# Block operands summed by an accumulating DMA from GpSimd instead of by VectorE, in a three-stage kernel on one Trainium2 core

## The chip, the core and the metric

The kernel runs on one core of a Trainium2 chip. The metric is device time in microseconds of one execution. Three runs of the kernel before gave 957.30, 958.35 and 959.70 us, a median of 958.35. One more execution was recorded by the profiler: it took 953.06 us, of which its trace spans 951.3.

## The reference

The program computes three stages in a row: linear attention with random features, a dense mixture of four experts (all tokens go through all experts, weighted by a probability), and a small second mixture with soft slots.

```python
# attention: q, k, v are (4, 8, 576, 64)
h = x @ omega.T - sum(x * x) / 2;  phi = exp(h - max(h)) / sqrt(128)
kv = phi(k).T @ v;  num = phi(q) @ kv;  den = phi(q) @ sum(phi(k))
x = num / (den + 1e-6)                   # then 2304 tokens x 512

# first mixture: w1 (4, 512, 1024), w2 (4, 1024, 512)
p = domain_probs / (domain_probs.sum(-1) + 1e-9)
for e in range(4):
    out += p[:, e:e+1] * (maximum(x @ w1[e], 0) @ w2[e])

# second mixture: 8 experts of 4 slots each
d = softmax over tokens of (out @ phi);  slots = d.T @ out
slot_out = maximum(slots @ w1[e], 0) @ w2[e] for each expert's slots
result = softmax over slots of (out @ phi) @ slot_out
```

All inputs and the output are float32.

## The kernel before

The middle stage takes most of the time: on TensorE it runs from about 152 us to about 890. It works in the type float32r. Each operand is kept as a high part and a low part (the rest that the high part leaves), and a product of two operands is three matmuls: high by high, high by low, low by high.

The work of this stage is cut into units. A unit is one of 8 weight groups (4 experts, 2 halves of the hidden layer each) with one of three blocks of 768 tokens: 24 units, numbered `u`, of weight group `G = u // 3` and block `b = u % 3`. From unit 3 on, the first layer and everywhere the second layer are done by a scheme with 7 products instead of 8 (the names I1, I2, I6, I5, I7, I3, I4 are the products in their order). Each product is 12 matmuls of 128 x 128 by 128 x 384. In units 0, 1 and 2 the first layer is done plainly, with 8 products (`plain1`), because the 7-product scheme needs four combined operands of each token block that are not there yet.

These combined operands are prepared beside the plain units, from the four sub-blocks of each token block, named `KH[0]` to `KH[3]`. For each block there are three sorts of step:

- W (`whole`): the high and low parts of a sub-block are added, to give it as one float32 array, `blocks[b, kh]` of 128 x 768. Four per block.
- T (`block_sum`): four differences of sub-blocks, in place, on VectorE. T 0 needs KH[0] and KH[2].
- S (`block_split`): the result is split again into a high part (cast on ScalarE) and a low part (a subtraction on VectorE), and both go to DRAM (`xt`) two ticks later, by two DMAs that ScalarE issues. Four per block.

The order is written out by hand. TensorE alternates a first-layer product of unit `u` (`plain1` or `product1`) with a second-layer product of unit `u - 1` (`product2`), and after each of them the table in `prep_steps` is asked for steps. Its key is `(u, n)`: even `n` is behind the matmuls of first-layer product `n / 2` of unit `u`, odd `n` behind second-layer product `(n - 1) / 2` of unit `u - 1`. A step that the table puts there is queued at that point on its engine. All engines take their instructions in order, so a step that waits holds up all that is queued behind it on that engine.

On VectorE the steps stand between the evacuations: ReLU with the token's weight (`scaled`, L595), the combinations of the hidden layer (L665, L734), its low parts (`split_low`, L659), and the sums of second-layer products (`evacuate2`, L806). ScalarE casts the high parts (L655) and copies some second-layer products out of PSUM (L808). GpSimd combines the weights (`weight_sum`, L419) and forms their low parts behind ScalarE's casts (`weight_split`, L437 and L438). SP issues the loads: operands `x` (L462) go three ahead through a ring of three buffers, so that a load waits until the operand three places earlier has been read by all its readers.

In the kernel before, W has two forms. For block 0, `fetch` loads the high and the low parts with eight DMAs from SP, near the end of attention, and VectorE adds them (L501). For blocks 1 and 2, VectorE adds the two halves of the operand that the ring holds for the plain products (L498), so those additions are readers of the ring's buffers too.

Of the kernel before, what the change touches and what calls it, by code (L numbers as in the profile page):

```python
# [9 lines left out]
F32 = mybir.dt.float32  # L10
F32R = mybir.dt.float32r
AF = mybir.ActivationFunctionType
ALU = mybir.AluOpType
# [4 lines left out]
B, H, S, D = 4, 8, 576, 64  # L18
# [22 lines left out]
def f32(ap):  # L41
    return ap.bitcast(F32)
# [3 lines left out]
def body(ctx: ExitStack, tc: tile.TileContext, ql, kl, vl, om, dp, wl, phi, w2l, out):  # L46
    nc = tc.nc
# [20 lines left out]
    def bank(tag, name):  # L68
        g = groups[tag]
        turns[tag] = turns.get(tag, -1) + 1  # L70
        n = g[turns[tag] % len(g)]
        return banks[n].tile([P, 512], F32, name=name, tag=f"k{n}", bufs=1)
# [29 lines left out]
    xd = [[dram.tile([P, 2, 2, NP, 2 * P], F32R, name=f"xd{b}_{h}") for h in range(2)] for b in range(XB)]  # L102
# [214 lines left out]
    def step(i):  # L317
        if i + 4 < n_seq:
            load(i + 4)
        to_dram()  # L320
        kind = seq[i][0] if i < n_seq else ""
        if begun(i, "q") and begun(i - 1, "q"):
            kind = "qq"
        for n in orders[kind].split():
            if n == "W":
                if early:
                    early.pop(0)()
                continue
            f, lag, kinds, *rest = work[n]
            if n == "P1" and i in (1, 2):  # L330
                keep_warm(10 if i == 1 else 7, "d")
            if begun(i - lag, *kinds) and not (n == "S" and i == 0):
                f(i - lag, *rest)
            if n == "M0" and i == 0:
                squares(0)
        if i == 0:
            split(2)
            split(3)
# [33 lines left out]
    I1, I2, I6, I5, I7, I3, I4 = range(7)  # L372
    w1s, w2s, hs, xs_, stage, lo_t, acc1, acc2, blocks, x2 = {}, {}, {}, {}, {}, {}, {}, {}, {}, []
# [14 lines left out]
    spare = [w1e.tile([P, 4, 2 * TH], F32, name="whole0", tag="w1x")]  # L388

    def raw_load(which, G):  # L390
        c = slice(0, DM) if which == "w1" else slice(DM, 2 * DM)
        r = stg.tile([P, 2, 2, 2, HD], F32, name=f"raw{which}", tag="raw")
        nc.sync.dma_start(
            out=r.rearrange("p j a h d -> p (j a) (h d)"),
            in_=wl[G * GJ:(G + 1) * GJ, :, c].rearrange("j p c -> p j c"),
        )
        stage[which, G] = r, stg.tile([P, 4, 2, HD], F32, name=f"T{which}", tag="T")
# [25 lines left out]
    def plain_terms():  # L423
        r, _ = stage["w1", 0]
        stage["w1", 0] = {i: r[:, :, k, m, :] for i, (k, m) in PLAIN.items()}
# [19 lines left out]
    def htile(i, lo, dt=F32R):  # L445
        n = HT[i] + ("l" if lo else "h")
        return hp.tile([P, 2 * TH], dt, name=n, tag=n)

    def three(t):
        return t.rearrange("p (a c) -> p a c", a=NP)  # L450
# [17 lines left out]
            load_operand(*ring[n])  # L468

    KH = ((0, 0), (1, 0), (0, 1), (1, 1))  # L470
    lows = {}

    def fetch():
        for n, (kh, i) in enumerate(zip(KH, (I5, I6, I3, I4))):
            k, half = kh
            blocks[0, kh] = spare[0][:, n]
            lows[kh] = htile(i, 1, F32)
            src = xd[0][half][:, k]
            nc.sync.dma_start(out=three(blocks[0, kh]), in_=f32(src[:, 0]))
            nc.sync.dma_start(out=three(lows[kh]), in_=f32(src[:, 1]))  # L480

    def place(b, kh):
        k, half = kh
        if b == 1:
            if kh == (0, 0):
                stage["xr"] = x2p.tile([P, 4, 2 * TH], F32, name="xr", tag="x2_2")
            blocks[b, kh] = stage["xr"][:, 2 * half + k]
        else:
            if k == 0:
                stage["xr", half] = prep.tile([P, 4, 512], F32, name="xr", tag=f"pre{half}")  # L490
            blocks[b, kh] = stage["xr", half].rearrange("p a c -> p (a c)")[:, k * 2 * TH:(k + 1) * 2 * TH]

    def whole(b, kh):
        if b:
            place(b, kh)
            hi, lo = xs_[b, kh]
            out = three(blocks[b, kh])
            nc.vector.tensor_tensor(out=out, in0=f32(hi), in1=f32(lo), op=ALU.add)  # L498
        else:
            a = blocks[b, kh]  # L500
            nc.vector.tensor_tensor(out=a, in0=a, in1=lows[kh], op=ALU.add)  # L501

    def block_sum(b, n):
        b11, b21, b12, b22 = (blocks[b, kh] for kh in KH)
# [30 lines left out]
        after(2, ("xt", b, i), keep)  # L535

    def prep_steps():
        W, T, S = whole, block_sum, block_split
        return {
            (0, 6): [(W, 0, KH[0])],  # L540
            (0, 8): [(W, 0, KH[1])],
            (0, 10): [(W, 0, KH[2]), (W, 0, KH[3])],
            (0, 12): [(T, 0, 0), (T, 0, 1)],
            (0, 14): [(T, 0, 2), (T, 0, 3)],
            (1, 4): [(W, 1, KH[0])],
            (1, 5): [(S, 0, I6)],
            (1, 6): [(W, 1, KH[1])],
            (1, 7): [(W, 1, KH[2])],
            (1, 8): [(W, 1, KH[3])],
            (1, 9): [(S, 0, I5)],  # L550
            (1, 10): [(T, 1, 0)],
            (1, 11): [(S, 0, I7), (T, 1, 1)],
            (1, 12): [(S, 0, I4)],
            (1, 13): [(T, 1, 2)],
            (2, 4): [(W, 2, KH[0])],
            (2, 6): [(W, 2, KH[1])],
            (2, 7): [(T, 1, 3)],
            (2, 8): [(W, 2, KH[2])],
            (2, 9): [(S, 1, I5)],
            (2, 10): [(S, 1, I4)],  # L560
            (2, 11): [(W, 2, KH[3])],
            (2, 12): [(S, 1, I7)],
            (2, 13): [(S, 1, I6)],
            (3, 5): [(T, 2, 0)],
            (3, 6): [(T, 2, 1)],
            (3, 7): [(T, 2, 2)],
            (3, 8): [(T, 2, 3)],
            (3, 13): [(S, 2, I6)],
            (4, 6): [(S, 2, I5)],
            (4, 7): [(S, 2, I7)],  # L570
            (4, 12): [(S, 2, I4)],
        }

    steps = prep_steps()

    def prep_one(u, n):
# [5 lines left out]
    def load_share(u):  # L582
        G, b = units[u]
        t = prb[u] = (
            prep.tile([P, 2, TH], F32, name="prb", tag=f"prb{u % 2}") if u else
            htile(I4, 0, F32).rearrange("p (a t) -> p a t", a=2)
        )
        nc.sync.dma_start(
            out=t.rearrange("p a (n t) -> p (a n) t", n=NP),
            in_=prd[TB * b:TB * b + TB, GROUPS[G][0], :].partition_broadcast(P),  # L590
        )
# [261 lines left out]
    for i in range(n_seq + 5):  # L853
        step(i)
        if i == 2:
            nc.sync.dma_start(out=phis, in_=phi.rearrange("(k p) s -> p k s", p=P))
            nc.vector.tensor_reduce(out=psum, in_=pr, axis=AX.X, op=ALU.add)
            nc.vector.tensor_scalar_add(psum, psum, 1e-9)
            nc.vector.reciprocal(out=psum, in_=psum)
            nc.vector.tensor_tensor(out=pr, in0=pr, in1=psum.to_broadcast([P, NT, E]), op=ALU.mult)  # L860
        if i == 3:
            tp = bank("d", "prt")
            nc.tensor.transpose(tp[0:NT * E, 0:P], pr.rearrange("p t e -> p (t e)"), ident)
            prs = pa.tile([P, P], F32, name="prs", tag="prs", bufs=1)
            nc.scalar.copy(out=prs[0:NT * E], in_=tp[0:NT * E, 0:P])
            nc.sync.dma_start(out=prd.rearrange("t e p -> (t e) p"), in_=prs[0:NT * E])
        if i == 14:
            load_share(0)
        if i == 19:
            raw_load("w1", 0)  # L870
            plain_terms()
        if 20 <= i < 20 + GJ:
            weight_split("w1", 0, (I1, I2, I6, I4)[i - 20])
        if i == 24:
            raw_load("w2", 0)
        if i == last_key + 2:
            groups.update({"b": [3, 4, 5], "c": [6]})
        if i == n_seq - 4:
            for n in range(3):
                load_operand(*ring[n])  # L880
        if i == n_seq - 2:
            fetch()
        if i == n_seq - 1:
            pa1.release()
            w2p = pool("w2p")
            lt = pool("lt")
            for n in range(4):
                weight_sum("w2", 0, n)
            groups.update({"b": [3, 4], "d": [5], "c": [6]})
            psH.release()  # L890
            pp["1"] = pool("ps1", space=PSUM, side="right")
        if n_seq <= i:
            for o in range(2 * (i - n_seq), min(7, 2 * (i - n_seq + 1))):
                weight_split("w2", 0, o)
# [189 lines left out]
    n = NB - 1  # L1084
# [243 lines left out]
```

## Time and profile before

| what | us |
|---|---|
| median of three runs | 958.35 (957.30 to 959.70) |
| profiled execution, whole | 953.06 |
| its span in the trace | 951.3 |
| TensorE busy | 932.7 (98%) |
| VectorE busy | 752.3 (79%) |
| ScalarE busy | 428.5 (45%) |
| GpSimd busy | 353.7 (37%) |
| chain that ended last | TensorE 86%, VectorE 6%, DMA 3%, ScalarE 2% |

An engine's busy time is the sum of its instructions, with overlaps counted once. TensorE is busy nearly all the time, so the end is set by its work and by the places where it stands still. Those places are found in the timeline of TensorE, where a bracket behind a row gives the idle time before it and the instruction that ended it. The granted TensorE clock is 1.00 of full speed in every stretch from 140 to 850 us, so it plays no part in units 0 to 5.

### The profile page before, as it was taken

The numbers are of one execution on the slowest core, as the hardware profiler recorded it, in microseconds if no ns is written. First come the engines' busy times: TensorE is split into PE (matmuls) and PEld (weight loads), VectorE is DVE, ScalarE is ACT, GpSimd is POOL, SyncE is SP. The second block draws the span as 40 slices with busy tenths as digits, with TensorE's granted clock in tenths as the row PEclk, the third lists the DMA queues.
The fourth block names the chain that finished last, engine by engine and source line by source line (L and its number), as shares of the span: only waits on it lengthen the run. The fifth ranks groups of instructions, "written<-read, shape, count | busy, mean of one in ns | idle before, by whom it ended". The sixth has DMA issues, their size and how long they took to land.

```text
span 951.3 us, 15807 instructions
## 1 busy us (share of the span) xinstructions
PE 932.7 (98%) x6065; PEld 888.9 (93%) x6065; DVE 752.3 (79%) x1134; ACT 428.5 (45%) x841; POOL 353.7 (37%) x290
## 2 busy tenths in 40 slices
PE   8999999999999999999999999999999999999997
PEld 7999989999999999999999999999999999997544
DVE  7788885999998878888888888788888888876432
ACT  4899885335543334334244334343342433325322
POOL 7877872432452341434043423414250534000000
PEclk9999999999999999999999999999999999999998
DMA  7678767684968776887767666767667677747897
GB/s 254 220 238 308 246 219 238 193 300 140 350 219 298 242 244 210 303 264 256 247 212 243 211 230 206 253 212 251 210 228 239 216 249 223 272 154 287 354 419 284
DMA packets 82111, 236.51 MB, mean 249 GB/s; under 512 B 8749, under 2 KB 36597, under 8 KB 77941
## 3 DMA queue, kind: packets, MB, share of 16 engines
q1 hardware_dynamic: 78292, 225.29, 69.2%
q10 hardware_dynamic: 3744, 10.23, 2.8%
q8 instruction: 48, 0.79, 0.3%
q14 instruction: 27, 0.21, 0.1%
HBM read 211.86 MB, written 23.63 MB: 248 GB/s over the span
## 4 chain that ended last, share of the span: by engine, by line
PE 86%; DVE 6%; DMA 3%; ACT 2%; issue 1%; SPq 0%; ACTq 0%; DVEq 0%
PE X L608 19%; PE X L784 18%; PE B L608 15%; PE B L784 14%; PE kv L221 3%; PE num L245 3%; PE pj L177 2%; PE so L1188 2%; PE tp L235 2%; PE pj L178 2%; PE pj L179 2%; PE hq L1160 1%; DMA raw<-kl 1%; DVE x L806 1%; DMA x<-xt 1%
## 5 line engine op out<-in xcount | busy, mean ns | idle before, releaser
L806 DVE TENSOR_TENSOR x<-X,x 128x768 f32<-128x768 f32 x84 | 80.0, 952 | 42.0 <-PE X L784 42.0
L419 POOL TENSOR_TENSOR Tw<-raww 128x512 f32<-128x512 f32 x30 | 41.3, 1397 | 192.5 <-DMA raww<-wl 192.5
L608 PE MATMUL X<-x,w1h 128*128 128x384 f32 x432 | 110.2, 335 | 0.2 <-PE B L784 0.2
L608 PE MATMUL B<-x,w1h 128*128 128x384 f32 x432 | 109.9, 335 | 0.0
L608 PE MATMUL X<-x,w1x 128*128 128x384 f32 x504 | 94.2, 334 | 0.6 <-DMA x<-xt 0.6
L608 PEld LDWEIGHTS X<-x,w1x 128*128 128x128 f32 x504 | 87.9, 188 | 0.9 <-ACT u L690 0.9
L202 ACT ACTIVATE fe<-pj,nb 128x128 f32<-128x128 f32 x288 | 82.7, 390 | 8.3 <-DVE nb L195 6.6
L655 ACT CAST s3h<-X 128x768 fp32r<-128x768 f32 x21 | 16.8, 802 | 147.7 <-DVE X L665 138.4
L608 PEld LDWEIGHTS X<-x,w1h 128*128 128x128 f32 x432 | 77.6, 188 | 0.8 <-PE B L784 0.5
L608 PEld LDWEIGHTS B<-x,w1h 128*128 128x128 f32 x432 | 77.8, 188 | 0.0
L608 PE MATMUL B<-x,w1l 128*128 128x384 f32 x216 | 72.2, 334 | 0.0
L608 PE MATMUL X<-x,w1l 128*128 128x384 f32 x216 | 72.2, 334 | 0.0
L806 DVE TENSOR_TENSOR x<-B,x 128x768 f32<-128x768 f32 x72 | 68.3, 949 | 3.3 <-PE B L784 2.8
L438 POOL TENSOR_TENSOR w2l<-raww,w2h 128x512 fp32r<-128x512 f32 x24 | 37.1, 1560 | 80.1 <-ACT w2h L437 80.1
L679 ACT COPY u<-X 128x768 f32<-128x768 f32 x63 | 50.1, 795 | 23.8 <-PE X L608 23.6
L185 DVE TENSOR_REDUCE stat<-pj 128x4 f32<-128x512 f32 x72 | 49.5, 687 | 12.7 <-PE pj L179 11.9
L438 POOL TENSOR_TENSOR w2l<-Tw,w2h 128x512 fp32r<-128x512 f32 x32 | 46.5, 1464 | 30.0 <-ACT w2h L437 30.0
L152 POOL TENSOR_TENSOR lo<-raw,hi 128x512 fp32r<-128x512 f32 x35 | 44.7, 1276 | 21.3 <-ACT hi L149 20.6
L438 POOL TENSOR_TENSOR w1l<-raww,w1h 128x512 fp32r<-128x512 f32 x25 | 38.0, 1524 | 36.6 <-ACT w1h L437 36.6
L655 ACT CAST e11h<-B 128x768 fp32r<-128x768 f32 x21 | 16.8, 801 | 77.0 <-PE B L784 68.5
L438 POOL TENSOR_TENSOR w1x<-Tw,w1x 128x512 fp32r<-128x512 f32 x21 | 27.7, 1317 | 57.4 <-ACT w1x L437 57.4
L608 PE MATMUL B<-x,w1x 128*128 128x384 f32 x252 | 47.1, 334 | 0.2 <-DMA x<-xt 0.2
(260 smaller groups left out, 2749.6 us busy)
## 6 DMA issues: line engine op xcount, KB each, us to landing
x<-xt SPq DMA_DIRECT2D x84, 768.0 KB, 5.3
x<-xd SPq DMA_DIRECT2D x75, 768.0 KB, 4.7
raww<-wl SPq DMA_DIRECT2D x16, 1024.0 KB, 6.8
w2tb<-w2l SPq DMA_DIRECT2D x11, 1024.0 KB, 9.6
raw<-ql SPq DMA_DIRECT2D x18, 512.0 KB, 5.0
xd<-xst SPq DMA_DIRECT2D x36, 256.0 KB, 3.0
prb<-prd SPq DMA_DIRECT2D x23, 384.0 KB, 6.6
raw<-kl SPq DMA_DIRECT2D x16, 512.0 KB, 5.8
```

What stands on the lines that cost most here:

```text
L152: (nc.gpsimd if i else nc.vector).tensor_tensor(out=lo, in0=r, in1=f32(hi), op=ALU.subtract)
L185: nc.vector.tensor_reduce(out=stats(i)[:, 4 * g:4 * g + 4, 0], in_=pjs[i, g], axis=AX.X, op=ALU.max)
L202: nc.scalar.activation(out=feats[i][:, 4 * g + h, :], in_=pjs[i, g][:, h, :], func=AF.Exp, bias=biases[i, g][:, h:h + 1], scale=1.0,)
L221: nc.tensor.matmul(kvps[b][h // 4][:, h % 4, :], lhsT=feats[i][p0:p0 + np_, h, :], rhs=v[p0:p0 + np_, h, :], start=first and h % 4 == 0, s ...
L245: nc.tensor.matmul(num[p0:p0 + n, h, :], lhsT=fts[i][:, 4 * g + h, p0:p0 + n], rhs=kvt[b][:, 4 * g + h, :], start=True, stop=True,)
L419: nc.gpsimd.tensor_tensor(out=out_, in0=a, in1=b_, op=op)
L438: nc.gpsimd.tensor_tensor(out=lo, in0=src, in1=f32(hi), op=ALU.subtract)
L608: nc.tensor.matmul(o, lhsT=lhs[:, jp, c], rhs=rhs[:, :, k, :], start=first and not k and not n, stop=False, skip_group_check=True,)
L655: nc.scalar.copy(out=pair(hs[i][0]), in_=src)
L679: nc.scalar.copy(out=pair(tmp({I1: "u1", I6: "u2", I5: "u4"}[i])), in_=q)
L784: nc.tensor.matmul(q[:, c, :], lhsT=lhs[:, jp, cs], rhs=rhs[:, jp, :], start=i in (I1, I2, I7) and jp == 0 and m == 0, stop=False, skip_gr ...
L806: nc.vector.tensor_tensor(out=o, in0=q, in1=o, op=ALU.add)
```

## The change

The sum of the high and the low part is now made by a DMA. For each sub-block, SP loads the high part from DRAM into the block's place (`fetch`, now for all three blocks), and then GpSimd issues a DMA that adds the low part, read from DRAM, onto it. VectorE's twelve additions are gone, and so is the second reader of the ring. For block 0 four loads by SP become four by GpSimd; for blocks 1 and 2 there are eight loads by SP and eight accumulating ones by GpSimd that did not exist.

```diff
+    def fetch(b, kh):
+        place(b, kh)
+        nc.sync.dma_start(out=three(blocks[b, kh]), in_=f32(xd[b][kh[1]][:, kh[0], 0]))
+
     def whole(b, kh):
-        if b:
-            place(b, kh)
-            hi, lo = xs_[b, kh]
-            out = three(blocks[b, kh])
-            nc.vector.tensor_tensor(out=out, in0=f32(hi), in1=f32(lo), op=ALU.add)
-        else:
-            a = blocks[b, kh]
-            nc.vector.tensor_tensor(out=a, in0=a, in1=lows[kh], op=ALU.add)
+        nc.gpsimd.dma_start(
+            out=three(blocks[b, kh]), in_=f32(xd[b][kh[1]][:, kh[0], 1]), accum_op=ALU.add
+        )
...
-            (0, 12): [(T, 0, 0), (T, 0, 1)],
-            (0, 14): [(T, 0, 2), (T, 0, 3)],
+            (0, 8): [(T, 0, 0)],
...
+            (1, 0): [(L, 1, KH[0]), (L, 1, KH[1])],
+            (1, 3): [(W, 1, KH[0]), (W, 1, KH[1])],
...
         if i == n_seq - 2:
-            fetch()
+            for kh in KH:
+                fetch(0, kh)
```

The table of steps is written anew for units 0 to 4. L is the new step of loading. T of block 0 goes from (0, 12) and (0, 14) to (0, 8), (0, 10), (0, 12) and (0, 14), one each. S of block 0 goes from (1, 5), (1, 9), (1, 11), (1, 12) to (1, 2), (1, 4), (1, 6), (1, 8); S of block 1 from (2, 9) to (2, 13) to (2, 4) to (2, 10); three of the four T of block 2 from unit 3 into unit 2; S of block 2 from (3, 13) to (4, 12) to (3, 9) to (4, 11). Lines below the steps have numbers lower by 6 or 7 in the changed kernel.

VectorE at the end of unit 0, before. `whole_171` is the place of block 0, L501 is W, L506 is T, L595 takes the last two plain products out of PSUM:

```order
L501 TENSOR_TENSOR whole_171<-whole_171,s4l 128x768
L501 TENSOR_TENSOR whole_171<-whole_171,e22l 128x768
L595 SCALAR_TENSOR_TENSOR r_2877<-X_2839,e22h 128x768
L659 TENSOR_TENSOR e11l<-u_2729,e11h 128x768
L506 TENSOR_TENSOR whole_171<-whole_171 128x768 x2
L272 TENSOR_TENSOR xst<-tpx,xst 128x512
L506 TENSOR_TENSOR whole_171<-whole_171 128x768 x2
L595 SCALAR_TENSOR_TENSOR u_2934<-B_2898,e22h 128x768
```

And the same place now, where T is L497 and the evacuation L588:

```order
L497 TENSOR_TENSOR whole_171<-whole_171 128x768
L588 SCALAR_TENSOR_TENSOR r_2871<-X_2834,e22h 128x768
L652 TENSOR_TENSOR e11l<-u_2725,e11h 128x768
L497 TENSOR_TENSOR whole_171<-whole_171 128x768
L272 TENSOR_TENSOR xst<-tpx,xst 128x512
L497 TENSOR_TENSOR whole_171<-whole_171 128x768
L588 SCALAR_TENSOR_TENSOR u_2926<-B_2892,e22h 128x768
```

Both W are gone from in front of the evacuation of `r`, and of the four T between it and that of `u`, two are left.

VectorE in unit 3, before. `xr` is the place of block 2, L506 is T, and `s4l` is the low part that the second-layer product I3 of unit 2 reads:

```order
L506 TENSOR_TENSOR xr<-xr 128x768
L659 TENSOR_TENSOR e22l<-r_3454,e22h 128x768
L665 TENSOR_TENSOR r_3724<-B_3711,u_3679 128x768
L595 SCALAR_TENSOR_TENSOR r_3724<-r_3724,prb 128x768
L506 TENSOR_TENSOR xr<-xr 128x768
L659 TENSOR_TENSOR s4l<-s_3378,s4h 128x768
```

And now, where T is L497:

```order
L497 TENSOR_TENSOR xr<-xr 128x768
L727 TENSOR_TENSOR s_3387<-s_3387,s_3535 128x768
L652 TENSOR_TENSOR e22l<-r_3467,e22h 128x768
L658 TENSOR_TENSOR r_3725<-B_3712,u_3682 128x768
L588 SCALAR_TENSOR_TENSOR r_3725<-r_3725,prb 128x768
L652 TENSOR_TENSOR s4l<-s_3387,s4h 128x768
```

One T of block 2 is left in unit 3, ahead of all of these, and none stands directly in front of `s4l`.

GpSimd from the end of unit 0 to unit 2, before. `sumr` is a small constant, `Tw` and `raww` are weights, `w1x` and `w1l` their low parts:

```order
L1077 COPY sumr<-ident 32x128 x4
L419 TENSOR_TENSOR Tw_3140<-raww_3138 128x512 x2
L419 TENSOR_TENSOR Tw_3140<-Tw_3140,raww_3138 128x512
L419 TENSOR_TENSOR Tw_3140<-raww_3138,Tw_3140 128x512
L438 TENSOR_TENSOR w1x<-Tw_3140,w1x 128x512 x2
L438 TENSOR_TENSOR w1l<-Tw_3140,w1h 128x512
L438 TENSOR_TENSOR w1x<-Tw_3140,w1x 128x512
L438 TENSOR_TENSOR w1l<-raww_3138,w1h 128x512 x3
```

And now, with the accumulating DMAs (L490), each of which waits for the load of its high part:

```order
L1071 COPY sumr<-ident 32x128 x4
L490 DMA xr<-xd_0_102 128x768 x2
L490 DMA xr<-xd_1_103 128x768 x2
L419 TENSOR_TENSOR Tw_3148<-raww_3146 128x512 x2
L419 TENSOR_TENSOR Tw_3148<-Tw_3148,raww_3146 128x512
L419 TENSOR_TENSOR Tw_3148<-raww_3146,Tw_3148 128x512
L438 TENSOR_TENSOR w1x<-Tw_3148,w1x 128x512
L490 DMA xr<-xd_0_104 128x768 x2
L438 TENSOR_TENSOR w1x<-Tw_3148,w1x 128x512
L490 DMA xr<-xd_1_105 128x768 x2
L438 TENSOR_TENSOR w1l<-Tw_3148,w1h 128x512
L438 TENSOR_TENSOR w1x<-Tw_3148,w1x 128x512
```

Four DMAs stand ahead of the weight sums of unit 1, and four more among the weight splits of unit 2.

## Rows read from the trace of the kernel before

**Rows 1.** The page, part 1: busy us of each engine, share, instructions.

```profile
PE 932.7 (98%) x6065; PEld 888.9 (93%) x6065; DVE 752.3 (79%) x1134; ACT 428.5 (45%) x841; POOL 353.7 (37%) x290
```

**Rows 2.** Timeline of TensorE: start, duration, instruction; each unit's first second-layer matmul.

```profile
177.72 0.33 PE L784 MATMUL X<-e11h,w2h 128*128 128x384 f32 x1
...
210.98 0.33 PE L784 MATMUL X<-e11h,w2h 128*128 128x384 f32 x1
...
242.18 0.33 PE L784 MATMUL X<-e11h,w2h 128*128 128x384 f32 x1
...
274.51 0.33 PE L784 MATMUL X<-e11h,w2h 128*128 128x384 f32 x1
...
304.09 0.33 PE L784 MATMUL X<-e11h,w2h 128*128 128x384 f32 x1
...
334.11 0.33 PE L784 MATMUL X<-e11h,w2h 128*128 128x384 f32 x1
```

**Rows 3.** Timeline of TensorE: rows with idle time before them, units 1 and 3.

```profile
187.12 0.45 PE L784 MATMUL X<-s2h,w2h 128*128 128x384 f32 x1 [0.91 <-ACT x L808]
...
192.15 0.44 PE L784 MATMUL X<-s1h,w2h 128*128 128x384 f32 x1 [0.57 <-ACT x L808]
...
253.53 2.32 PE L608 MATMUL X<-x,w1x 128*128 128x384 f32 x12 [0.64 <-DMA x<-xt]
...
266.43 0.44 PE L784 MATMUL X<-s4l,w2h 128*128 128x384 f32 x1 [1.51 <-DVE s4l L659]
```

**Rows 4.** Timeline of all engines, from unit 0 to unit 1.

```profile
170.69 1.95 DVE L501 TENSOR_TENSOR whole<-whole,s4l 128x768 f32<-128x768 f32 x1
...
172.56 2.05 DVE L501 TENSOR_TENSOR whole<-whole,e22l 128x768 f32<-128x768 f32 x1
...
175.30 0.34 PE L608 MATMUL B<-x,w1l 128*128 128x384 f32 x1
...
180.58 0.95 DVE L595 SCALAR_TENSOR_TENSOR u<-B,e22h 128x768 f32<-128x768 f32 x1
...
183.55 0.84 ACT L655 CAST s3h<-u 128x768 fp32r<-128x768 f32 x1 [11.43 <-DVE u L665]
...
186.28 0.79 ACT L808 COPY x<-X 128x768 f32<-128x768 f32 x1
...
187.93 2.76 POOL L1077 COPY sumr<-ident 32x128 f32<-32x128 f32 x4
```

**Rows 5.** Groups by line, VectorE, 175 to 300: count, busy us, mean ns.

```profile
L506 DVE TENSOR_TENSOR xr<-xr 128x768 f32<-128x768 f32 x8 | 11.1, 1393 | 0.0
...
L498 DVE TENSOR_TENSOR xr<-x 128x768 f32<-128x768 f32 x8 | 9.8, 1221 | 0.0
```

**Rows 6.** Waits of SP's queue: us in total, times, longest us.

```profile
SPq L462 <- DVE xr L498: 36.7, 7, 10.9
```

**Rows 7.** Timeline of GpSimd in unit 2.

```profile
221.64 1.42 POOL L438 TENSOR_TENSOR w1x<-Tw,w1x 128x512 fp32r<-128x512 f32 x1 [9.21 <-ACT w1x L437]
223.71 1.32 POOL L438 TENSOR_TENSOR w1x<-Tw,w1x 128x512 fp32r<-128x512 f32 x1 [0.65 <-ACT w1x L437]
228.88 1.72 POOL L438 TENSOR_TENSOR w1l<-Tw,w1h 128x512 fp32r<-128x512 f32 x1 [3.85 <-ACT w1h L437]
230.91 1.65 POOL L438 TENSOR_TENSOR w1x<-Tw,w1x 128x512 fp32r<-128x512 f32 x1 [0.31 <-ACT w1x L437]
237.95 1.78 POOL L438 TENSOR_TENSOR w1l<-raww,w1h 128x512 fp32r<-128x512 f32 x1 [5.40 <-ACT w1h L437]
```

**Rows 8.** Windows: length, busy us per engine, clock, DMA share, GB/s.

```profile
180.00:240.00 60.00, 58.52 (x336) 57.88 (x335) 57.95 (x57) 26.10 (x36) 19.25 (x14) 1.00 0.63 205
240.00:260.00 20.00, 19.20 (x109) 18.43 (x108) 18.39 (x17) 12.07 (x17) 7.04 (x5) 1.00 0.99 376
```

**Rows 9.** Line L479, SP's 384 KB loads: issue (ns, min/median/max) and landing.

```profile
L479 SPq DMA_DIRECT2D whole<-xd x4: 439/482/502, 142.6 to 145.8; - x4
...
DMA to landing us min/median/max: 4.3/6.0/8.0
```

More of the change, by code (lines that the diff above doesn't have):

```diff
@@ L470, in body @@
     KH = ((0, 0), (1, 0), (0, 1), (1, 1))
[L471 to L480, printed above, removed]
     def place(b, kh):
         k, half = kh
-        if b == 1:
+        if b == 0:
+            blocks[b, kh] = spare[0][:, KH.index(kh)]
+        elif b == 1:
             if kh == (0, 0):
@@ L537, in prep_steps @@
     def prep_steps():
-        W, T, S = whole, block_sum, block_split
+        L, W, T, S = fetch, whole, block_sum, block_split
         return {
-            (0, 6): [(W, 0, KH[0])],
-            (0, 8): [(W, 0, KH[1])],
-            (0, 10): [(W, 0, KH[2]), (W, 0, KH[3])],
-            (0, 12): [(T, 0, 0), (T, 0, 1)],
-            (0, 14): [(T, 0, 2), (T, 0, 3)],
[L545 to L569, printed above, removed]
@@ new lines, in prep_steps @@
+            (0, 0): [(W, 0, KH[0]), (W, 0, KH[1])],
+            (0, 2): [(W, 0, KH[2]), (W, 0, KH[3])],
+            (0, 8): [(T, 0, 0)],
+            (0, 10): [(T, 0, 1)],
+            (0, 12): [(T, 0, 2)],
+            (0, 14): [(T, 0, 3)],
+            (1, 0): [(L, 1, KH[0]), (L, 1, KH[1])],
+            (1, 1): [(L, 1, KH[2]), (L, 1, KH[3])],
+            (1, 3): [(W, 1, KH[0]), (W, 1, KH[1])],
+            (1, 2): [(S, 0, I6)],
+            (1, 5): [(W, 1, KH[2]), (W, 1, KH[3])],
+            (1, 4): [(S, 0, I5)],
@@ new lines, in prep_steps @@
+            (1, 7): [(T, 1, 0)],
+            (1, 6): [(S, 0, I7)],
+            (1, 9): [(T, 1, 1)],
+            (1, 8): [(S, 0, I4)],
+            (1, 11): [(T, 1, 2)],
+            (1, 13): [(T, 1, 3)],
+            (2, 2): [(L, 2, KH[0]), (L, 2, KH[1])],
+            (2, 3): [(L, 2, KH[2]), (L, 2, KH[3])],
+            (2, 4): [(S, 1, I5)],
+            (2, 5): [(W, 2, KH[0]), (W, 2, KH[1])],
+            (2, 6): [(S, 1, I4)],
+            (2, 7): [(W, 2, KH[2]), (W, 2, KH[3])],
+            (2, 8): [(S, 1, I7)],
@@ L570, in prep_steps @@
+            (2, 9): [(T, 2, 0)],
+            (2, 10): [(S, 1, I6)],
+            (2, 11): [(T, 2, 1)],
+            (2, 13): [(T, 2, 2)],
+            (3, 5): [(T, 2, 3)],
+            (3, 9): [(S, 2, I6)],
+            (4, 5): [(S, 2, I5)],
             (4, 7): [(S, 2, I7)],
-            (4, 12): [(S, 2, I4)],
+            (4, 11): [(S, 2, I4)],
         }
```

## The prediction, made before the changed kernel was run

> **What bounds the kernel now.** I read the page's busy times first: TensorE is busy 98% of the span, VectorE 79%, GpSimd 37% [rows 1]. So a microsecond saved elsewhere counts only where TensorE stands still for it. The change acts in units 0 to 4, so I read TensorE's timeline there. A unit shows best as the distance between its first second-layer matmul and the next unit's [rows 2]. Units with 15 products can be read off from 210.98 to 242.18: 31.20 us, 2.08 a product, so 14 products take 29.12. The other distances, each against its ideal, are 33.26 (31.20, lost 2.06), 32.33 (29.12, lost 3.21), 29.58 (lost 0.46) and 30.02 (lost 0.90). All that TensorE loses between 178 and 334 us is 6.63 us, 0.70% of 953.06. That is the ceiling of the gain; behind it, TensorE's rows follow on each other without idle time until the last stage.
>
> Then I looked for what ended the losses. In unit 1 they are two waits for ScalarE's copy L808, 0.91 and 0.57 idle; in unit 3 one of 1.51 for VectorE's `s4l` and one of 0.64 for an operand load [rows 3]. The rest of the 6.63 is time around such stops. The copies of unit 1 go back to VectorE [rows 4]: the last plain product of unit 0 ends at 175.64 (175.30 and 0.34), but VectorE takes it out of PSUM at 180.58, 4.94 us late. ScalarE waits 11.43 us for what follows from it (`s3h`), and the copy L808 stands behind that in ScalarE's queue, at 186.28. VectorE is busy 57.95 of the 60 us from 180 to 240 [rows 8]: in units 1 and 2 it is all but the bound, and it enters unit 3 with work left over.
>
> **The change part by part.**
>
> *VectorE, unit 0.* The two W directly before the evacuation of `r`, 1.95 and 2.05 us [rows 4], go, and two of the four T after it move ahead, to where TensorE is not waiting. One T alone costs 0.95, which I take from L595, an operation of that size [rows 4]. Two moved T are 1.9, so 4.00 + 1.9 = 5.9 us leave the stretch against a lag of 4.94: the last evacuation follows TensorE directly. ScalarE's copy then waits for its own product, which ends 2.08 after 177.72, at 179.80, and is done by 180.6, over 5 us before TensorE wants it. What is late next there: nothing I can name. Of the 2.06 I take 1.8.
>
> *VectorE, units 1 and 2.* Eight W go, 9.8 us [rows 5]; three T (1.39 each beside GpSimd's work, same rows) come from unit 3 into unit 2 and one leaves unit 2 for unit 1. Unit 2 has 7 steps on VectorE instead of 9, unit 1 8 instead of 11.
>
> *VectorE, unit 3.* `s4l` loses the T before it, and two more T before that: about 4 us, against 1.51 idle. The evacuation of `r` in front of it cannot start before its product ends; then come two operations of 0.95 and `s4l`, 0.95 to 2.05, so 2.9 to 4.0 us, while TensorE needs two more products (4.16) and two matmuls before it reads `s4l`. It fits, narrowly. The load that was late is `x<-xt`: from 240 to 260 the DMA engines are busy 0.99 [rows 8]. S of block 1 moves ahead by some 4 products (8 us), so its 3.1 MB of stores leave this window; and the operand loads no longer wait for VectorE, which was 36.7 us in 7 waits, the longest 10.9 [rows 6]. Of the 3.21 I take 2.4.
>
> *Units 4 and 5.* S of block 2 moves by one to four places. Of 0.46 and 0.90 I take 0.5 together.
>
> *GpSimd.* No DMA from GpSimd is in the trace. Its time on the engine is bounded below by SP's issue of such a load, 0.48 us, and above by 8.0, the longest landing [rows 9], if the engine were held until the data is there. I take 1.3, the shortest tensor instruction of this engine here [rows 7]. In unit 0 the engine has nothing else to do at that place. In unit 1 the four W start once `sumr` is through, at 190.69 less the 4.94 [rows 4], 185.8, and once the new loads have landed; I put that at 188. Behind them stand weight sums with time to spare. In unit 2, with 223.06 the end of the first split, the queue is through at 223.06 + 4 W + 1.32 + 1.72 + 1.65 = 227.75 + 4 W, and the next split, `w1l` of I1, cannot start before 237.95, when ScalarE's cast releases it [rows 7]. So up to W = 2.55 us each the four are free; at 1.3 the spare time is 5 us.
>
> *VectorE waits for the accumulated data.* This is new: T waits for a DMA. With W at 1.3, KH[2] of block 1 is issued at 188 + 2.6 = 190.6 and lands 4.3 to 8.0 us later [rows 9], 194.9 to 198.6. T 0 stands behind the third of three operations that follow a product which ended at 191.58 [rows 3], less the stop of 0.91 that is gone: 190.67 + 2.85 = 193.5. VectorE would wait 1.4 to 5.1 us. It and the eight operations of 0.95 queued behind it take 8.6 us up to the unit's last evacuation, whose product ends one product before 210.98 [rows 2], less the 1.48 of idle that is gone, at 207.4; so T 0 can start as late as 198.8 before that one is late. In unit 2 the same wait is 3 to 7 us, with a lag at its end of up to 1.5; 4.94 of lag cost 2.06, so 1.5 costs 0.6. I take 0.5 for both, 0 to 2 as bounds.
>
> *DMA.* Sixteen transfers of 384 KB are added, 6.3 MB, in the 60 us from 180, which carry 12.3 MB (205 GB/s) at a share of 0.63 [rows 8]. In proportion the share becomes 0.63 x 18.6 / 12.3 = 0.95; if an accumulating transfer counts twice, 1.11. The ring loads three operands ahead, and a plain operand serves two products, so I take no cost, with up to 3.6 as the bound (a rival below).
>
> Sum: -1.8 - 2.4 - 0.5 + 0.5 = -4.2. The profiled execution would go from 953.06 to 948.9. The runs shown have a median of 958.35, 5.3 above it; I take the same 4.2 off: 954.1.
>
> **Two rules of the Trainium skill.** The rows show VectorE's two-input additions at 0.95 alone and up to 2.05 where GpSimd works too [rows 4, 5]. The Trainium skill (SBUF — State Buffer, SBUF: two separate sides, and Who interferes with whom) speaks of an exclusive lock: GpSimd cannot write DMA descriptors while VectorE holds the shared ports, though it infers that `tensor_tensor` doesn't block them. If it did, each W would wait for one more VectorE instruction, which makes 1.3 + 0.95 = 2.25 us, still under 2.55; two instructions would break it. That is the first rival, and this rule is why I don't give it less.
>
> The Trainium skill (DMA: Bandwidth & Descriptors, Anatomy of one DMA) fits a GpSimd DMA by 2.0 us plus its bytes over 436 GB/s, which as an estimate is 2.9 us for 384 KB. By that T 0 would not wait, and the sum would be -4.7 instead of -4.2; no run here shows it yet, and I keep the landing times of the rows.
>
> **The rivals.**
>
> *GpSimd's queue becomes the bound (slower).* If a W holds the engine longer than 2.55 us, by its issue or by waiting for a load that lands late, `w1l` of I1 is late by 4 x (W - 2.55), and TensorE stands in front of unit 3. At W = 6.0, the median landing, that is 13.8 us, less the 4.2: 963 profiled, 968 in the runs' terms. It is slower than before from W = 3.6 on. For it: nothing in the trace prices this instruction. Against it: the shortest and the longest rows leave 2.55 in the lower part only if the engine waits for landing, and it need not.
>
> *The accumulated data is late.* If landing takes twice the 8.0, T 0 is 13 us late and unit 1 ends with a lag like the one of unit 0; it costs 2.06 there and as much in unit 2, and the gain is nearly gone: 958.
>
> *Operand loads become the bound.* With a share at 0.99, one 20 us window lost 0.64 of idle and about 1.2 with what is around it. Three such windows are 3.6: a gain of 1.1, 957.2.
>
> *VectorE's relief is not what TensorE waits for.* The stops of units 3 to 5 stay and only unit 1's go: 956.5.
>
> **How the numbers follow.** About 0.3%, 2.9 us, is what a measurement of this kernel can tell from no change. The forecast, a gain of 2.9 to 6.6 (951.7 to 955.4), has 0.57. The three that end within 2.9 of before have 0.28 together, most of it on the second and third; the first, slower, 0.15. With the forecast's 4.2 between ceiling and bound, the range goes from 951.3, just past the ceiling, to 960.5, which takes in the cases without gain and the mild ones of the first rival and leaves out its far end. Faster 0.57, same 0.28, slower 0.15.
>
> **What would show it.** Right: the five distances between units at 31.2, 31.2, 29.1 to 29.9, 29.1 to 29.6 and 29.1 to 30; the last evacuation of unit 0 within 1 us of its product; no wait of SP for VectorE's W; `s4l` out of TensorE's waits. Wrong: a GpSimd row or gap of over 2.5 us at a W in unit 2 with TensorE waiting for `w1l`; VectorE waiting over 6 us at a T for a DMA; TensorE waiting for `x<-xd` or `x<-xt` in units 1 to 3.

## The result: slower, and the profile after

The changed kernel took 965.62 us (median of 6 runs, 964.37 to 972.21), the kernel before beside it 958.18 (6 runs, 957.30 to 959.70): a ratio of 1.0085, 95% interval 1.0056 to 1.0114. The forecast was 954.1 with a range up to 960.5, so it was wrong in sign and the time lies outside the range.

The profiled execution took 966.77 us, 13.71 more than that of before. The medians differ by 7.44 only: before's profiled execution was 5.1 below the median of its runs, this one 1.2 above. Before's executions differ with the granted clock of TensorE: of 30 more that were taken for e5 to e8, the three with a mean of 0.997 took 953.48 to 956.40 us and the one with 0.987 took 965.45; its profiled execution had 0.997. So the rows below say where the time went, and the medians how much it is.

The busy times of the changed kernel, as in [rows 1]:

```profile
PE 939.3 (97%) x6065; PEld 894.1 (93%) x6065; DVE 737.2 (76%) x1122; ACT 428.6 (44%) x841; POOL 362.9 (38%) x302
```

VectorE lost 15.1 us of work, as meant, and still the span grew. TensorE's timeline, the rows that answer to [rows 2]:

```profile
177.82 0.33 PE L777 MATMUL X<-e11h,w2h 128*128 128x384 f32 x1
...
221.06 0.33 PE L777 MATMUL X<-e11h,w2h 128*128 128x384 f32 x1
...
254.21 0.34 PE L777 MATMUL X<-e11h,w2h 128*128 128x384 f32 x1
...
285.81 0.34 PE L777 MATMUL X<-e11h,w2h 128*128 128x384 f32 x1
...
314.93 0.33 PE L777 MATMUL X<-e11h,w2h 128*128 128x384 f32 x1
...
344.65 0.33 PE L777 MATMUL X<-e11h,w2h 128*128 128x384 f32 x1
```

The distances are 43.24, 33.15, 31.60, 29.12 and 29.72; against the same ideals the losses are 12.04, 1.95, 2.48, 0 and 0.60, 17.07 in place of 6.63. That is 10.44 of the 13.71. Another 3.16 come behind 344.65: in the last stage TensorE's granted clock fell to 0.66 from 910 to 920 us, where before it was 1.00. It does not take the accumulating DMAs to see that: the profiles of e1 and e5 below, in which blocks 1 and 2 are not accumulated, have 0.67 from 900 to 910. Unit 1 alone lost 10 us more than before. VectorE's timeline there (a bracket is idle time and what ended it; T is L497, the evacuation L799):

```profile
196.97 0.96 DVE L652 TENSOR_TENSOR e12l<-s,e12h 128x768 fp32r<-128x768 f32 x1
209.05 0.96 DVE L497 TENSOR_TENSOR xr<-xr 128x768 f32<-128x768 f32 x1 [11.12 <-DMA xr<-xd]
209.93 0.95 DVE L652 TENSOR_TENSOR e22l<-r,e22h 128x768 fp32r<-128x768 f32 x1
210.80 0.95 DVE L520 TENSOR_TENSOR whole<-whole,xh 128x768 fp32r<-128x768 f32 x1
211.67 0.95 DVE L799 TENSOR_TENSOR x<-B,x 128x768 f32<-128x768 f32 x1
```

The first T of block 1 waits 11.12 us for the accumulated data, and the evacuation of a second-layer product, which needs none of that data, stands three places behind it. TensorE waits for this evacuation, and has waited before for a copy and for an operand:

```profile
191.17 0.44 PE L777 MATMUL X<-s1h,w2h 128*128 128x384 f32 x1 [0.70 <-ACT x L801]
...
200.38 1.01 PE L601 MATMUL X<-x,w1h 128*128 128x384 f32 x2 [2.70 <-DMA x<-xd]
201.19 0.52 PE L601 MATMUL X<-x,w1l 128*128 128x384 f32 x1
...
207.98 0.34 PE L601 MATMUL B<-x,w1l 128*128 128x384 f32 x1
212.67 0.69 PE L777 MATMUL B<-e22h,w2h 128*128 128x384 f32 x1 [4.36 <-DVE x L799]
...
216.35 0.52 PE L777 MATMUL B<-e22l,w2h 128*128 128x384 f32 x1
216.68 0.73 PE L601 MATMUL B<-x,w1h 128*128 128x384 f32 x2
```

After the two longer stops the matmuls last 0.52 us instead of 0.34, and the granted clock is 0.51 and 0.50 (the windows of 200 and 212 below): TensorE runs at the lower of its two levels, 1.2 GHz instead of 2.4. The product from 212.67 to 216.68 takes 4.0 us instead of 2.08, the one from 200.38 to 203.99 3.6. Stops of 2.70, 4.36 and 0.70, and 3.4 of slow products, make 11.2 of the 12.04.

Why the data came late is in the chain of waits (start, us, what), the part before that T:

```profile
183.40 9.45 DMA xr<-xd
...
193.20 0.86 POOL xr L490
...
194.21 14.75 DMA xr<-xd
...
209.05 0.96 DVE xr L497
```

The load that took 9.45 us is that of KH[1]; the second accumulating DMA waits for it. The third, that of KH[2], goes out behind the second and takes 14.75. GpSimd's timeline shows its four accumulating DMAs of block 1:

```profile
191.40 0.88 POOL L490 DMA_DIRECT2D xr<-xd  x1 [4.26 <-DMA xr<-xd]
193.20 0.86 POOL L490 DMA_DIRECT2D xr<-xd  x1 [0.92 <-DMA xr<-xd]
194.21 0.86 POOL L490 DMA_DIRECT2D xr<-xd  x1 [0.15 <-issue]
201.00 0.88 POOL L490 DMA_DIRECT2D xr<-xd  x1 [5.93 <-issue]
```

The first two go out as the loads of their high parts land, the third right behind the second. The fourth comes 5.93 us after the third, and "issue" says that it waited for nothing that the profile shows. The windows (columns as in [rows 8]) show the DMA engines full:

```profile
190.00:195.00 5.00, 4.30 (x25) 3.98 (x24) 2.59 (x3) 2.68 (x4) 2.53 (x3) 1.00 1.03 413
...
200.00:203.00 3.00, 2.62 (x8) 2.62 (x9) 0.00 (x0) 0.00 (x0) 0.88 (x1) 0.51 1.06 296
...
205.00:210.00 5.00, 3.32 (x20) 3.00 (x18) 0.95 (x2) 0.00 (x0) 0.00 (x0) 1.00 1.07 298
...
212.00:217.00 5.00, 4.33 (x14) 4.33 (x15) 3.39 (x5) 0.80 (x1) 1.75 (x2) 0.50 0.62 254
```

From 200 on they are as full as at 190 (share 1.06 against 1.03), but move 296 GB/s and not 413: what they do there takes longer per byte. VectorE and ScalarE do nothing from 200 to 203.

In unit 2 the first T of block 2 waits as well, 7.16 us, and the fourth accumulating DMA there waits 5.54. That unit loses 1.95 us.

### The profile page after: what moved, and what is told of

The parts are those of the page before. It is cut to its first block, busy times and chain, and to the rows that moved or that the text cites. A ratio compares the mean times of both kernels' runs of the same rounds, so it can differ in the third digit from the quotient of the medians.

```text
span 965.0 us, 15823 instructions
## 1 busy us (share of the span) xinstructions
PE 939.3 (97%) x6065; PEld 894.1 (93%) x6065; DVE 737.2 (76%) x1122; ACT 428.6 (44%) x841; POOL 362.9 (38%) x302
## 4 chain that ended last, share of the span: by engine, by line
PE 82%; DVE 5%; DMA 5%; POOL 2%; issue 2%; ACT 1%; SPq 1%; ACTq 0%; POOLq 0%; DVEq 0%
PE X L777 18%; PE X L601 18%; PE B L777 14%; PE B L601 13%; DMA xr<-xd 4%; PE kv L221 3%; PE num L245 3%; PE hq L1154 2%; PE so L1182 2%; PE pj L177 2%; PE tp L235 2%; PE pj L178 1%; PE pj L179 1%; POOL lo L152 1%; PE tpm L937 1%
## 5 line engine op out<-in xcount | busy, mean ns | idle before, releaser
L799 DVE TENSOR_TENSOR x<-X,x 128x768 f32<-128x768 f32 x84 | 80.0, 952 | 42.4 <-PE X L777 42.1
L648 ACT CAST s3h<-X 128x768 fp32r<-128x768 f32 x21 | 16.8, 802 | 146.4 <-DVE X L658 146.4
L799 DVE TENSOR_TENSOR x<-B,x 128x768 f32<-128x768 f32 x72 | 68.3, 949 | 5.3 <-PE B L777 4.8
L648 ACT CAST e11h<-B 128x768 fp32r<-128x768 f32 x21 | 16.8, 801 | 77.4 <-PE B L777 68.5
L177 PE MATMUL pj<-om_hi,hi 128*128 128x256 f32 x144 | 45.6, 317 | 2.3 <-ACT fe L202 2.1
```

What stands on the lines that cost most here:

```text
L177: nc.tensor.matmul(o, lhsT=hi[:, pi, :], rhs=om_hi, start=True, stop=False)
L648: nc.scalar.copy(out=pair(hs[i][0]), in_=src)
L799: nc.vector.tensor_tensor(out=o, in0=q, in1=o, op=ALU.add)
```

## Experiments

Each kernel is told by its edit; "before" is the kernel before, run beside it on the same chip. L, W, T and S are the steps, the number behind them the block.

**e1: the moves without the DMA.** T and S stand at about the new places, but VectorE adds, as before, and so W stands ahead of them. Against the kernel before only the table is another:

```diff
-            (0, 12): [(T, 0, 0), (T, 0, 1)],
...
-            (1, 5): [(S, 0, I6)],
...
-            (1, 10): [(T, 1, 0)],
...
+            (0, 8): [(W, 0, KH[3]), (T, 0, 0)],
...
+            (1, 2): [(S, 0, I6)],
...
+            (1, 9): [(T, 1, 0)],
```

> VectorE adds the parts again as in the kernel before (no accumulating DMA, no new loads), but the steps T and S stand at the changed kernel's places as far as the operands allow (T of block 1 two places later). Theory A (accumulated data lands late, because the DMA engines are overfull in unit 1): without that data nothing is late, so the time is at or a little under the kernel before, 952 to 959, unit 1 no more than 33.3 us long. Rival B (the moved steps do the harm, by stores that collide with operand loads): slower than before, 962 or more, with TensorE waiting for x<-xd in unit 1.

957.24 us against 957.27, ratio 0.9993 (0.9974 to 1.0011). The moved steps neither cost nor gain. In the profile the five distances lose 4.65 us in place of 6.63, but unit 1 begins 2.2 us later than before, behind a stop of TensorE of 2.11 for VectorE.

**e2: the DMA without the moves.** The changed kernel with the table of before; L at (1, 0), (1, 1), (2, 2), (2, 3).

```diff
-            (1, 3): [(W, 1, KH[0]), (W, 1, KH[1])],
+            (1, 4): [(W, 1, KH[0])],
+            (1, 6): [(W, 1, KH[1])],
...
-            (1, 7): [(T, 1, 0)],
+            (1, 10): [(T, 1, 0)],
```

> The accumulating DMAs and the new loads stay, but W, T and S stand at the places of the kernel before (T of block 1 three places or some 6 us later, the stores of block 0 some 4 places later). Theory A: the data has 6 us more and less traffic beside it, so VectorE's wait at the first T of block 1 falls from 11.1 us to 0 to 5, unit 1 from 43.2 us to 31 to 36, time 952 to 960. Rival B: equal to before, since no step is moved: 957 to 959.5, with no wait at T either way. If the DMA is slow in itself whatever the traffic: the wait stays over 6 us and the time over 961.

965.30 against 957.27, ratio 1.0089 (1.0066 to 1.0112): as slow as the changed kernel, though T came later. It loses the time at other places: the first T of block 1 waits 5.2 us and not 11.1, but two T of block 0 now wait too, 3.4 and 2.8; unit 1 is 39.89 long, and in units 1 and 2 TensorE waits 4.3 us for plain operands and 2.9 for ScalarE's copies. So the wait at one T is not all of it. With e1 this puts the cause in the DMAs.

**e3: a copy in place of the sum.**

```diff
-            out=three(blocks[b, kh]), in_=f32(xd[b][kh[1]][:, kh[0], 1]), accum_op=ALU.add
+            out=three(blocks[b, kh]), in_=f32(xd[b][kh[1]][:, kh[0], 1])
```

> The changed kernel, but GpSimd's DMAs copy the low part instead of adding it (the sum is left out, the block's place holds the low part alone); same bytes, same queue, same places. Theory A with the adding as its main part (an adding byte holds the DMA engines 1.8 times as long as a plain one: 2.6% of the span for 4.72 MB against 68.3% for 226.86 MB): landing falls from 11.8 us in the median to 6 to 9, the wait at T from 11.1 to under 6, time 957 to 961. Theory A with the added traffic alone as its cause, or any cause in GpSimd's queue: landing and time stay, 963 to 968.

956.43 against 957.27, ratio 0.9993 (0.9974 to 1.0012). The same loads, the same twelve GpSimd DMAs of 384 KB, each behind the load of its high part as in the changed kernel, and the slowdown is gone: it hangs on the adding. GpSimd's queue in part 3 of the page (packets, MB, share of 16 engines), first of the changed kernel:

```profile
q0 software_dynamic: 1728, 4.72, 2.6%
```

and with the copy:

```profile
q0 software_dynamic: 960, 4.72, 1.4%
```

2.6% of 965.0 us on 16 engines is 25.1 us, 2.09 for each of 12 DMAs; with the copy 1.4% of 952.2 is 13.3, 1.11 each. For the same bytes an accumulating DMA has 144 packets instead of 80 and holds the DMA engines 1.9 times as long. The number of packets alone is not the reason, since SP's loads of 384 KB have 144 too (part 3 has 576 more on SP's queue for the four loads more). In the trace of the changed kernel a packet of 3072 bytes took 252 ns in the median in the accumulating DMAs, 121 ns in SP's loads. A window with the copy:

```profile
200.00:205.00 5.00, 4.90 (x29) 4.58 (x27) 1.99 (x3) 0.00 (x0) 0.00 (x0) 1.00 1.03 413
```

The engines are still full at 200, but at 413 GB/s, and the first T of block 1 waits 4.9 us, not 11.1. Unit 1 is 35.23 long, 1.97 more than before, so even without the adding this scheme costs something there.

**e4: half the room for descriptors.** A descriptor tells a DMA engine what to move; those of GpSimd's DMAs are written to a buffer of 1024 bytes, here of 512.

```diff
-    nc = bacc.Bacc(..., dynamic_dma_scratch_size=1024)
+    nc = bacc.Bacc(..., dynamic_dma_scratch_size=512)
```

> The changed kernel with half the scratch for GpSimd's DMA descriptors (512 instead of 1024 bytes). In the trace of the changed kernel the fourth of each four DMAs stands 3.0, 5.9 and 5.5 us on GpSimd, until about when the first has landed, as if three had room at a time. Rival C (room for descriptors sets when W is issued): now the second or third of four waits too, each by some 4 to 10 us, and T waits over 15 us, time 970 or more. Theory A without the room as a part of it: gaps and time unchanged, 963 to 968.

985.44 against 957.27 (six runs, 978.65 to 993.57), ratio 1.0274 (1.0225 to 1.0324, without the longest). GpSimd's timeline at block 1:

```profile
197.43 0.88 POOL L490 DMA_DIRECT2D xr<-xd  x1 [4.92 <-DMA xr<-xd]
207.87 0.88 POOL L490 DMA_DIRECT2D xr<-xd  x1 [9.56 <-issue]
```

Now the second one waits for the first: one accumulating DMA has room, where three had. So the 5.93 before the fourth is a wait for room. More room was not tried.

**e5: block 0 alone.** Only block 0 accumulates, with the new places of unit 0; from unit 1 on all is as before.

```diff
+    ACC = (0,)
+
     def whole(b, kh):
-        if b:
+        if b in ACC:
+            nc.gpsimd.dma_start(
+                out=three(blocks[b, kh]), in_=f32(xd[b][kh[1]][:, kh[0], 1]), accum_op=ALU.add
+            )
+        else:
             place(b, kh)
...
```

> Only block 0 is summed by the accumulating DMAs, with the changed kernel's unit 0; blocks 1 and 2 are added by VectorE, and all steps from unit 1 on stand as in the kernel before. Theory A (the harm is accumulated data that T of blocks 1 and 2 reads too early): no harm is left, the 4.94 us of lag at the end of unit 0 are gone, unit 1 is 31.2 to 31.8 us long instead of 33.26, time 954 to 957.3. Rival D (GpSimd's DMAs cost something wherever they stand): 959 or more.

955.95 against 958.90, ratio 0.9964 (0.9941 to 0.9986). Unit 1 is 31.20 long, its ideal: the 2.06 of [rows 2] comes back whole. Unit 3 is 33.88 in this profile, 1.55 longer than before, so that the five distances together lose 6.05 in place of 6.63. The gain of 2.95 between the medians is thus not read off from the distances.

**e8: blocks 1 and 2 alone.** VectorE adds block 0 at before's places.

```diff
     def whole(b, kh):
+        if b == 0:
+            a = blocks[b, kh]
+            nc.vector.tensor_tensor(out=a, in0=a, in1=lows[kh], op=ALU.add)
+            return
         nc.gpsimd.dma_start(
...
```

> Block 0 is summed by VectorE as in the kernel before (both parts loaded by SP), blocks 1 and 2 as in the changed kernel. Theory A: all the harm is in blocks 1 and 2, and the relief in unit 0 is lost as well: 965 to 969, VectorE waits 8 us or more at the first T of block 1. Rival E (block 0's DMAs at the end of attention do the harm): at 957 to 960.

966.39 against 958.90, ratio 1.0084 (1.0055 to 1.0112); the T of blocks 1 and 2 wait 15.8 us in two waits. As slow as the changed kernel: blocks 1 and 2 are enough for the harm, and by e5 block 0 does none.

**e7: the stores of block 0 later.** The changed kernel with S of block 0 back at (1, 5), (1, 9), (1, 11), (1, 12), so that its stores leave the time of block 1's loads.

```diff
-            (1, 2): [(S, 0, I6)],
...
+            (1, 5): [(W, 1, KH[2]), (W, 1, KH[3]), (S, 0, I6)],
```

> The changed kernel with S of block 0 back at its places of before, so that the 3.1 MB of its stores leave about 6 us later and not between the loads and the accumulating DMAs of block 1. Theory A with the traffic beside the accumulating DMAs as a main part: the third of them lands in 7 to 10 us instead of 14.75, VectorE waits 2 to 6 us at the first T of block 1 instead of 11.1, unit 1 is under 37 us, time 957 to 962. With the adding itself and the late loads as the cause: the wait stays at 9 or more and the time at 963 to 968.

965.90 against 958.90, ratio 1.0084 (1.0051 to 1.0116); the first T waits 13.2 us. The stores are not what makes the data late. TensorE's stop for an operand in unit 1 is gone, that for the evacuation is 7.61 instead of 4.36.

**f3: the two parts that the first T needs come first.**

```diff
-            (1, 0): [(L, 1, KH[0]), (L, 1, KH[1])],
+            (1, 0): [(L, 1, KH[0]), (L, 1, KH[2])],
```

W goes in the same order.

> The changed kernel with one swap: of block 1, the parts that the first T needs are loaded and added first and second instead of first and third. Theory A: that T waits some 2 to 5 us less (6 to 9 instead of 11.1), time 959 to 964. If the wait is not for the order but for the overfull engines as a whole, no change: 964 to 968.

962.91 against 957.12, ratio 1.0062 (1.0038 to 1.0087). The longest wait falls from 11.1 to 8.2 us, and the interval overlaps that of the changed kernel: some of it at most.

**f1: later readers.** In addition T of block 1 goes to (1, 12), (1, 13), (2, 2), (2, 4), and block 2's steps are those of e6 below; all blocks accumulate.

```diff
-            (1, 7): [(T, 1, 0)],
+            (1, 12): [(T, 1, 0)],
```

> All three blocks are summed by the accumulating DMAs, as in the changed kernel, but their readers stand later: the first T of block 1 five products (10.4 us) later, the first of block 2 five or so later, and the two parts that the first T needs are loaded and added first. The added traffic is the same. Theory A in the form left by the runs so far (the reader is too early for data that lands late; nothing else is wrong): VectorE waits under 2 us in all, unit 1 is 31.2 to 33 us long, time 951 to 955. Rival F (the DMA engines, overfull in unit 1, make operand loads late whoever reads the sums): unit 1 still 35 us or more, TensorE waits for x<-xd, time 959 or more.

961.44 against 957.12, ratio 1.0042 (1.0023 to 1.0061). The waits of VectorE did not vanish, they moved with the T:

```profile
209.65 0.96 DVE L497 TENSOR_TENSOR xr<-xr 128x768 f32<-128x768 f32 x1 [3.64 <-DMA xr<-xd]
...
217.26 0.96 DVE L497 TENSOR_TENSOR xr<-xr 128x768 f32<-128x768 f32 x1 [5.02 <-DMA xr<-xd]
```

The second of them is for the fourth DMA, which waited 8.27 us on GpSimd and then took 10.94. Unit 1 is 32.74 long, 10.5 less than in the changed kernel and as the first theory had it, but in unit 2, 36.47 long, TensorE waits 3.4 us for a plain operand, and the time is that of rival F. Late data and late operand loads both cost here, and room in the order gives back only part.

**e6: blocks 0 and 2 accumulate, block 1 is added by VectorE, block 2 read late.**

```diff
+    ACC = (0, 2)
...
+            (2, 5): [(W, 2, KH[0]), (W, 2, KH[2])],
+            (2, 7): [(W, 2, KH[1]), (W, 2, KH[3])],
+            (3, 5): [(T, 2, 0)],
+            (3, 7): [(T, 2, 1)],
+            (3, 9): [(T, 2, 2)],
+            (3, 11): [(T, 2, 3)],
```

> Blocks 0 and 2 are summed by the accumulating DMAs, block 1 by VectorE. Block 2's first T comes 10 products after its loads are queued instead of 7 and needs the first two of four DMAs instead of the first and third, its four T stand in unit 3. Theory A: the data is there in time (VectorE waits under 1 us for a DMA), VectorE has four additions less in unit 2, time 952 to 956, under the kernel of block 0 alone or equal to it. Rival D: 960 or more, though no T waits.

952.87 (951.04 to 955.29) against 958.90, ratio 0.9938 (0.9918 to 0.9957): faster than both kernels. Its distances are 31.21, 31.34, 31.51, 29.71 and 29.72, a loss of 3.73 in all. The wait for room is still there:

```profile
224.47 0.86 POOL L493 DMA_DIRECT2D xr<-xd  x1
229.78 0.88 POOL L493 DMA_DIRECT2D xr<-xd  x1 [4.45 <-issue]
```

but no T waits for a DMA any more. The distances account for 2.9 of the 6.0 us between the medians. The rest goes with the granted clock: its median is 0.996 in these runs and 0.994 in those of before, and the three of each with 0.997 or more took 951.04 to 951.10 and 953.48 to 956.40. Why the clock is higher no run shows.

**f2: e6's steps, but VectorE adds block 2**, with W of block 2 at about the places of before.

```diff
-    ACC = (0, 2)
+    ACC = (0,)
```

> The steps of the kernel in which blocks 0 and 2 are accumulated, but block 2 is added by VectorE. If that kernel's gain over the one with block 0 alone (952.87 against 955.95) comes from VectorE's relief: 954.5 to 957, unit 3 over 31.5 us. If it comes from the moved steps alone: 952 to 954, unit 3 at 31.5 or less.

954.65 against 957.12, ratio 0.9971 (0.9957 to 0.9986), like e5. TensorE waits 3.6 us for `s4l` in unit 3, as in [rows 3] and longer (0.20 in e6), and unit 3 is 36.19 long. The medians, each against its own before, leave about 3 us of e6's gain to block 2's DMA, but the intervals of e6 and f2 touch; that is likely and not shown.

**e9: the copy, and the load on the DMA engines brought back.** e3, with eight more transfers of 384 KB that nobody reads, on SP's queue.

```diff
+        if b:
+            nc.sync.dma_start(out=more[4 * b - 4 + KH.index(kh)], in_=f32(xd[b][kh[1]][:, kh[0], 0]))
```

> GpSimd's DMA copies the low part instead of adding it (the sum is left out, as in the kernel with the copy), and behind each of the eight loads of blocks 1 and 2 SP issues one more transfer of the same 384 KB, from DRAM to DRAM, that nobody reads. A load of 384 KB held the DMA engines about 1.1 us, an accumulating transfer 2.09, so the eight more transfers bring the load of units 1 and 2 about to that of the changed kernel, while GpSimd's own DMAs stay short and find room for their descriptors. Theory A1 (the load on the DMA engines is what makes block 1 late, whoever causes it): unit 1 at 38 to 43 us instead of 35.2, VectorE waits 8 us or more at the first T of block 1, 961 to 967 us. Theory A2 (it is the adding transfer itself, by its descriptors, their room and its own latency): unit 1 at 34 to 36 us, the wait at the first T 4 to 6 us as with the copy alone, 954 to 958 us.

969.05 against 957.61, ratio 1.0110 (1.0091 to 1.0130), unit 1 45.38 long: slower than either theory had it, and not in the way of A1. The first T waits 2.5 us, and TensorE stands for an operand instead:

```profile
212.59 1.01 PE L604 MATMUL X<-x,w1h 128*128 128x384 f32 x2 [6.96 <-DMA x<-xd]
```

The window in which GpSimd's third copy of block 1 is issued:

```profile
200.00:205.00 5.00, 5.00 (x27) 5.00 (x27) 2.65 (x3) 1.62 (x3) 0.54 (x1) 0.87 1.01 405
```

The engines are as full, at 405 GB/s, and yet GpSimd's copies land no later than in e3 (least, median and longest 5.1, 7.1 and 10.2 us, in e3 4.9, 8.4 and 10.8). So load on the DMA engines alone did not make the block's data late. Nor does this run show that load alone made the kernel slow: SP issues the load of that operand at 199.24, 16.8 us into the unit, behind an added transfer of 8.96 us in its queue, where e3 issues it 10.0 us into the unit, and it then takes 13.30 us.

## Why the prediction was wrong, point by point

**The failed step: "VectorE waits for the accumulated data ... I take 0.5 for both, 0 to 2 as bounds."** The place was right. VectorE came to the T at 197.9, 4.4 after the 193.5 of the prediction but inside the limit of 198.8 that it worked out, and KH[2] was issued at 194.21, 3.6 after its 190.6. What failed is the landing: 4.3 to 8.0 us, taken from plain loads at a quiet place [rows 9]. The twelve accumulating DMAs took this (the summary of line L490, us):

```profile
DMA to landing us min/median/max: 6.3/9.5/14.8
```

and the one that decides took 14.75. With the copy the longest is 10.8 (e3). The upper bound held only for a DMA of the same kind on engines as free as those of [rows 9]. The prediction also set a sentence beside this term: by the Trainium skill (DMA: Bandwidth & Descriptors, Anatomy of one DMA) such a DMA would take an estimated 2.9 us. The trace does not agree; not even the quickest, 6.3, comes near, nor does the quickest copy, 4.9 (e3).

**"DMA ... I take no cost, with up to 3.6 as the bound."** This failed with it. The prediction had written that the share becomes 0.95, or 1.11 if an accumulating transfer counts twice, and took no cost from either. It does count almost twice (2.09 against 1.11 us of engine time, e3). From 180 to 240 the share is 0.86, but in the windows from 190 to 210 shown above it is 1.03 to 1.07. An average over 60 us hid that the loads of block 1, the four sums, a weight load and block 0's stores meet within 20.

**The rival "the accumulated data is late".** This was the mechanism, with the wrong price: at most the gain, 958, never slower. It lacked two things. The two longer stops of TensorE cost more than their length, since the products after them run at the lower clock (3.4 us in unit 1). And the fourth DMA waits for descriptor room (5.93 us), so that the later T come later too.

**The rival "operand loads become the bound"** also took part: TensorE's 2.70 for `x<-xd`, and more where block 1's readers stand later (f1, 3.4). Its sum leaves out the 0.5 for the data: 4.2 less 3.6 is a gain of 0.6, not 1.1.

**The rival "GpSimd's queue becomes the bound".** It had the right side and the wrong cause. A W holds the engine 0.86 to 1.18 us, less than the 1.3 taken. What it waits for is loads and room, and behind it TensorE waited 0.7 us for `w1l` once, at the end of unit 2.

**"VectorE, unit 0", -1.8.** Right. The last evacuation of unit 0 starts at 177.13, 1.2 after its product (the sign was within 1), where it was 4.94 late; ScalarE's `s3h` starts at 180.09 instead of 183.55 [rows 4]. Alone (e5) the step returns the 2.06 of unit 1. In the changed kernel the gain drowns in the same unit.

**"VectorE, unit 3", -2.4; units 4 and 5, -0.5.** TensorE's wait for `s4l` fell from 1.51 to 0.69, but the distance is 31.60, a loss of 2.48 against 3.21: 0.7 gained, so the rival that VectorE's relief is not what TensorE waits for was partly right there. Unit 4 and 5 together lose 0.60 in place of 1.36, close to the 0.5 taken. SP's waits for VectorE's W [rows 6] are gone as forecast, and e1 shows what the moves bring by themselves: nothing that can be measured.

Of the signs named as wrong, VectorE's wait of over 6 us at a T came twice (11.12 and 7.16), TensorE's for `x<-xd` once (2.70), and a GpSimd gap of over 2.5 us at a W in unit 2 once (5.54), with the 0.7 for `w1l`.

Still open: how much of block 1's 14.75 us is the longer engine time and how much the descriptors' room. e3 takes both away, e4 shows that room matters, and e9 that full engines alone do not make a copy land so late. Open too is how much of the slowdown goes through the waiting T and how much through late operand loads: e2 and f1 lose their time partly at the second.

## What to carry to other kernels

Before work moves from an engine to the DMA, look at the DMA share in windows as short as the transfers take to land, not in an average of the stage, and count an accumulating DMA by its time on the DMA engines and not by its bytes. A late DMA costs what stands behind its reader in an in-order queue: put the reader behind everything TensorE waits for, which here (f1) gave back about half of the loss, or leave that block on the engine. Undoing a change block by block shows what of it pays: here block 0 did and block 2 likely did, and together (e6) they beat both kernels.

## What the runs showed of the hardware that was not expected

- An accumulating DMA of 384 KB took 144 packets and 2.09 us of all 16 DMA engines, a copy 80 packets and 1.11 us; a packet of 3072 bytes took 252 ns in the first and 121 in SP's loads. The issue of an accumulating DMA took GpSimd 0.86 to 1.18 us, that of a copy 0.54 to 0.71.
- With 1024 bytes for descriptors three accumulating DMAs of this size were on their way at a time, with 512 one; four copies went out at 1024 without such a wait.
- After stops of 2.70 and 4.36 us TensorE's matmuls took 0.52 us instead of 0.34 for about a product each, and the clock granted was 0.51 from 200 to 203 and 0.50 from 212 to 217. Stops of 1.51 and less [rows 3] were followed by none of that.
- In the last stage the granted clock fell to 0.66 for 10 us in the profile of the changed kernel, and to 0.67 in those of e1 and e5. The cause is open.
